# A state-space layer and a gated feed-forward in one kernel: the first loads, and the order of loads behind them, rearranged

## The chip, the cores and the metric

The kernel runs on one core of a Trainium2 chip. The metric is the device time of one execution in microseconds (us); of several runs the median counts. A core has five engines that run side by side, each with its own instruction queue: TensorE (PE in the profile, with its weight loads as PEld), VectorE (DVE), ScalarE (ACT), GpSimd (POOL) and SyncE (SP). Transfers between memory and the core are issued from SP, ACT or POOL and share 16 DMA engines.

## The reference

The first half is a chunked state-space layer over x [4 batches, 8 heads, 768 tokens, 32], a decay a per token, and B and C with 16 states per token. With L the causal products of decays inside a chunk, it computes:

```python
M = (C_chunk @ B_chunk.T) * L                       # chunk x chunk
y = M @ x_chunk + (C_chunk @ state) * exp(cum)      # inside, and from the state before
state = decay_full * state + (B_chunk * decay_from_j).T @ x_chunk
```

The heads are put side by side, which gives 3072 tokens of 256 features, and the second half is a gated feed-forward over d_ff = 1536:

```python
out = (np.maximum(y @ w_gate, 0) * (y @ w_val)) @ w_out
```

## The kernel before, in words

Tokens go through in 12 pairs of 128-token chunks (three pairs to a batch), and the feed-forward in 6 blocks of 512 tokens, two pairs to a block. The whole order is written out by hand: for each engine the last line (`in_order`, L798) chains the instructions in the order of the program text, so where a call stands in the text is where its instructions stand in each engine's queue.

The start. `a` is loaded as 64 rows (batch, head, half of the sequence) of 384 values, in two column pieces of 256 and 128 (L114 to L116, on SP). B and C of pair 0 are issued from ACT (`load_wide(0, nc.scalar)`, L117), x of pair 0 and B and C of pair 1 from SP behind a (L118, L119). A first activation (L122) brings ACT's table load. DVE, TensorE and POOL meanwhile set up zero tiles, identities and masks; `keep_warm(n)` (L159) issues n dummy matmuls on a zero tile, 14 of them first (L165). POOL issues the first six feed-forward weight transfers (L183 to L185; `weights(f0, f1)` brings columns f0 to f1, in units of 128, of w_gate and of w_val).

Decays are products, so `cp` is built by two multiplying scans over a, split at column 256 like the load (L189 to L193); the second scan starts from the first one's last value. `first_decay` (L217, called at L594) brings pair 0's decays to the token layout by matmuls that need only the first 256 columns. Then for pair 0: a reciprocal (L599), the scaling of B and of C by the decays (`first_scale`, L235, called at L600 and L601), dummies, the transposes of B and of C (`transp`, L323, called at L604 and L606), their copies out of PSUM (BT on ACT at L356, CT on DVE at L369), the matmul bu, which sorts B's rows (L608 to L611), the casts of x (L618), the scores (`G`, L371), their masking (`gevac`, L390), the state matmul (`astep`, L415) with its evacuation (`sevac`, L424), and the output (`first_y`, L439), from which the first feed-forward matmuls follow (`gvp`, L534; L544 is its matmul). The first state of pair 1 and the rest of pair 0 are computed in between.

Later pairs need their own factors: `wide_decay` (L198) is the matmul that brings them and `wide_factors` (L241) copies them and their reciprocals by DVE. `scale_bc` (L275) scales B and C on POOL and `cast_x` (L298) casts x. `load_wide(p, q, hold)` (L75) issues B and C of a pair; with `hold`, a one-element memset by DVE on the destination stands ahead of the transfers, and since they overwrite it, the queue waits with them until DVE has come that far. `load_x` (L87) issues x in two transfers and `load` (L97) all six of a later pair. Pairs 2 and 3 are loaded at L633 to L636, the last weights at L639 and L640, pairs 4 and 5 at L652.

PSUM is used through seven banks in turn (`bank`, L66), so a tile waits until the tile seven requests before it has been read. From `gvp(0, 0, 0)` (L642) on, feed-forward matmuls (`gvp`, `gv`, `gvh`, `fout`) are interleaved with the pieces of the next pairs.

Of the kernel before, what the change touches and what calls it, by code (L numbers as in the profile page):

```python
# [29 lines left out]
def kernel(  # L30
# [13 lines left out]
    nc = tc.nc  # L44
# [7 lines left out]
    NF = DF // 128  # L52
# [22 lines left out]
    def load_wide(p, q=nc.sync, hold=False):  # L75
        b, c0 = p // PPB, 2 * (p % PPB)
        sl = slice(c0 * 128, (c0 + 2) * 128)
        bcr = raw.tile([128, NH, 2, 2, N], FP32, tag="bcr", name="bcr")
        if hold:
            nc.vector.memset(bcr[0:1, 0, 0, 0, 0:1], 0.0)  # L80
        for src, j in ((B, 0), (C, 1)):
            q.dma_start(
                out=bcr[:, :, j].rearrange("p h r n -> p h (r n)"),
                in_=src[b, :, sl, :].rearrange("h (p r) n -> p h (r n)", r=2))
        st[p] = {"bcr": bcr}

    def load_x(p, hold=False):  # L87
        b, c0 = p // PPB, 2 * (p % PPB)
        xr = raw.tile([128, 2, NH, D], FP32, tag="xr", name="xr")
        if hold:  # L90
            nc.vector.memset(xr[0:1, 0, 0, 0:1], 0.0)
        for i in range(2):
            cs = slice((c0 + i) * 128, (c0 + i + 1) * 128)
            nc.sync.dma_start(out=xr[:, i], in_=x[b, :, cs, :].rearrange("h s d -> s h d"))
        st[p]["xr"] = xr
# [15 lines left out]
    H = S // 2  # L111
    HC = NC // 2
    a_sb = glob.tile([2 * BH, H], FP32)
    a_rows = a.rearrange("b h (w s) -> (b h w) s", w=2)  # L114
    for lo, hi in ((0, 256), (256, H)):
        nc.sync.dma_start(out=a_sb[:, lo:hi], in_=a_rows[:, lo:hi])  # L116
    load_wide(0, nc.scalar)  # L117
    load_x(0)  # L118
    load_wide(1)  # L119
    first = const.tile([1, 2], FP32)  # L120
    nc.vector.memset(first, 0.0)
    nc.scalar.activation(first[:, 1:2], first[:, 0:1], AF.Relu)  # L122
# [1 line left out]

    warm = const.tile([128, 256], BF16)
    nc.vector.memset(warm, 0.0)
    identf = const.tile([2 * BH, 2 * BH], FP32)
    make_identity(nc, identf)
    ident = const.tile([128, 128], BF16)
# [29 lines left out]
    def keep_warm(n, cols=256):  # L159
        w = bank("w")  # L160
        for _ in range(n):
            nc.tensor.matmul(out=w[:, 0:cols], lhsT=warm[:, 0:128], rhs=warm[:, 0:cols],  # L162
                             start=True, stop=True)
# [8 lines left out]
    def weights(f0, f1):  # L172
        fs = slice(f0 * 128, f1 * 128)
        for w, src in ((wg, moe_w_gate), (wv, moe_w_val)):
            nc.gpsimd.dma_start(
                out=w[:, :, fs], in_=src[:, fs].rearrange("(k p) f -> p k f", k=2))
# [12 lines left out]
    for lo, hi in ((0, 256), (256, H)):  # L189
        nc.vector.tensor_tensor_scan(  # L190
            out=cp[:, lo:hi], data0=a_sb[:, lo:hi],
# [6 lines left out]
    def wide_decay(ps):  # L198

        d = bank("wdec", (128, len(ps), 2, 8))  # L200
        first = True
        for k, p in enumerate(ps):
            b, c0 = p // PPB, 2 * (p % PPB)
            for i in range(2):
                w, o = (c0 + i) // HC, ((c0 + i) % HC) * 128
                for r in range(2):
                    nc.tensor.matmul(  # L207
                        out=d[64 * i:64 * i + 64, k, r],
                        lhsT=cp[:, o + r:o + 128:2], rhs=pick[:, w, 8 * b:8 * b + 8],
                        start=first or (k == 0 and r == 0), stop=True,  # L210
                        tile_position=(0, 64 * i), skip_group_check=True)
                first = False
        return d
# [27 lines left out]
    def wide_factors(ps, d):  # L241
        f = const.tile([128, len(ps), 2, 2, 8], FP32, name="wf%d" % ps[0])
        nc.vector.reciprocal(f[:, :, 0], d)
        nc.vector.tensor_copy(f[:, :, 1], d)
        for k, p in enumerate(ps):
            factors[p] = f[:, k].rearrange("p j r h -> p (j r) h")
# [27 lines left out]
    def scale(p, eng, ceng):  # L274
        scale_bc(p, eng)  # L275
        cast_x(p, ceng)

    def scale_bc(p, eng):
        b, c0 = p // PPB, 2 * (p % PPB)
        s = st[p]  # L280
        bs = att.tile([128, 4, 128], BF16, tag="bs", name="bs")
        if p < NWIDE:
            src = s["bcr"].rearrange("s h j r n -> s (j r) h n")
            f = factors[p]
        else:
            src = s["bcr"].rearrange("s i j h n -> s (i j) h n")
            f = scaleBC[:, b, c0:c0 + 2].rearrange("s c j h -> s (c j) h")
        eng.tensor_tensor(  # L288
            out=bs.rearrange("s k (h n) -> s k h n", h=NH), in0=src,
            in1=f.to_broadcast([128, 4, NH, N]), op=ALU.mult)  # L290
        if p < NWIDE:
            s["tin"] = [[bs[:, 2 * j + r] for r in range(2)] for j in range(2)]
            s["sort"] = s["tin"][0]
        else:
            s["tin"] = [[bs[:, 2 * i + j] for i in range(2)] for j in range(2)]
            s["B"] = s["tin"][0]
# [26 lines left out]
    def transp(p, k, apart=False):  # L323

        s = st[p]
        if "tp" not in s:
            s["tp"] = {}
        if apart and k == 1:
            s["tp"][k] = bank("tpc", (128, 2, 128), BF16)
        elif not s["tp"]:  # L330
            tp = bank("tp", (128, 2, 2, 128), BF16)
            s["tp"] = {0: tp[:, 0], 1: tp[:, 1]}
        for i in range(2):
            nc.tensor.transpose(out=s["tp"][k][:, i], in_=s["tin"][k][i], identity=ident)  # L334

    def tevac(p, beng, ceng):

        s = st[p]
        tp = s.pop("tp")
        s["BT"] = BT = att.tile([128, 2, 2, 128], BF16, tag="BT", name="BT")  # L340
        s["CT"] = CT = att.tile([128, 2, 128], BF16, tag="CT", name="CT")
        wide = p < NWIDE

        def tokens(k):
            src = tp[k]
            if wide:
                return src.rearrange("s r m -> s m r")
            return src.rearrange("s i m -> s (i m)")

        def rows(dst):  # L350
            dst = dst.rearrange("s i m -> s (i m)")
            return dst.rearrange("s (m r) -> s m r", r=2) if wide else dst

        if beng is nc.scalar:
            for t in range(2):
                nc.scalar.mul(rows(BT[:, t]), tokens(0), tmask[:, t:t + 1])  # L356
        else:
            src = tokens(0).unsqueeze(1)
            out_ = BT.rearrange("s t i m -> s t (i m)")
            if wide:  # L360
                shape = [128, 2, 128, 2]
                out_ = out_.rearrange("s t (m r) -> s t m r", r=2)
                mk = tmask.unsqueeze(2).unsqueeze(3)
            else:
                shape = [128, 2, 256]
                mk = tmask.unsqueeze(2)
            nc.vector.tensor_tensor(out=out_, in0=src.to_broadcast(shape),
                                    in1=mk.to_broadcast(shape), op=ALU.mult)
        (ceng.copy if ceng is nc.scalar else ceng.tensor_copy)(rows(CT), tokens(1))  # L369
# [45 lines left out]
    def astep(p, i):  # L415

        c = 2 * (p % PPB) + i
        if c == NC - 1:
            return
        nc.tensor.matmul(  # L420
            out=A_ps, lhsT=st[p]["B"][i], rhs=st[p]["x"][i],
            start=(c == 0), stop=(c == NC - 2), skip_group_check=True)
# [179 lines left out]
    s0["tin"] = [[bs0[:, 2 * j + r] for r in range(2)] for j in range(2)]  # L602
    keep_warm(5)
    transp(0, 0, True)  # L604
    keep_warm(1)
    transp(0, 1, True)  # L606
    tevac(0, nc.scalar, nc.vector)
    bu = bank("bu", (128, 128))  # L608
    for r in range(2):
        nc.tensor.matmul(out=bu, lhsT=order[:, 0, r], rhs=bs0[:, r],  # L610
                         start=(r == 0), stop=(r == 1))  # L611
    bxu = att.tile([128, 128], BF16, tag="bxu", name="bxu", bufs=1)
    nc.scalar.copy(out=bxu, in_=bu)
    s0["B"] = [bxu, None]
# [2 lines left out]
    for i in range(2):  # L617
# [3 lines left out]
    G(0)  # L621
    gevac(0, 4)
    astep(0, 0)
    d1 = wide_decay([1])
    keep_warm(5)
    sevac(0, 0)
    wide_factors([1], d1)
    scale_bc(1, nc.gpsimd)
    first_y()
    dm = first_mid()  # L630
    nc.vector.tensor_tensor(out=fB[:, 1], in0=fB[:, 0],
                            in1=dm.unsqueeze(1).to_broadcast([128, 2, 8]), op=ALU.mult)
    load_wide(2, nc.sync, True)  # L633
    load_x(2)
    load_wide(3)
    load_x(3)  # L636
    first_scale(0, fB[:, 1], bsm)
    s0["sort"] = [bsm[:, r] for r in range(2)]
    weights(6, 9)  # L639
    weights(9, NF)  # L640

    gvp(0, 0, 0)  # L642
    sort_b(0)
# [4 lines left out]
    astep(0, 1)  # L648
    sevac(0, 1)
    st.pop(0)  # L650
    cast_x(1, nc.gpsimd)
    for n in (4, 5):  # L652
        load(n, nc.sync)
    gvp(0, 0, 2)
    sort_evac(1)
    G(1)
# [2 lines left out]
    gevac(1, 3)  # L659
    sevac(1, 0)  # L660
    gvp_evac(*u)
    dall = decay()
    Dm(1)
    inter(1, 0)
# [2 lines left out]
    d2 = wide_decay([2, 3])  # L667
    yevac(1, nc.scalar)
    wide_factors([2, 3], d2)
    scale(2, nc.gpsimd, nc.gpsimd)  # L670
    sevac(1, 1)
    gvp(0, 1, 0)
# [156 lines left out]
```

## Time and profile before

| | |
|---|---|
| median of 3 runs | 129.77 us (129.56 to 132.0) |
| the profiled execution, its own time | 131.06 us |
| span of that execution in the profile | 129.4 us |
| mean granted clock of TensorE | 0.998 |
| TensorE busy | 124.6 us, 96% of the span |
| DVE, ACT, POOL busy | 88.0, 77.7 and 42.5 us |
| DMA | 12.11 MB, 94 GB/s in the mean |

The profile's times start at the span's beginning; 131.06 - 129.4 = 1.7 us of the execution lie outside the span. The chain of waits follows the work that ended last backwards, so a piece in it is one that the end waited for. The timeline lists instructions by start and length, with the idle time of the engine ahead of them and what ended it in brackets. Queues of DMA issues are written SPq, ACTq; L82 is line 82 of the kernel. Matmuls overlap, and their single lengths are longer than their distance.

### The profile page before, as it was taken

The page shows a single profiled execution, that of the slowest core. Times are in us where ns is not written, and L with a number is a line of the kernel's source. Part 1 is how long each engine was busy: PE and PEld are TensorE (multiplying, and loading weights), DVE is VectorE, ACT ScalarE, POOL GpSimd, SP SyncE. Part 2 cuts the span into 40 slices and gives each one's busy share as a digit, 9 for nine tenths or more (in the row PEclk, how much of TensorE's full clock was granted, in tenths as well). Part 3 has the DMA queues.
Part 4 walks back from the last instruction along what each step waited for, and adds up shares of the span by engine and source line. Part 5 has one row for each costly group of instructions (what it writes and reads, how often), then busy time and mean ns, then how long its engine had stood idle before and what let it go on. Part 6 is the DMA issues. An engine that isn't in the chain of part 4 may idle for free.

```text
span 129.4 us, 3381 instructions
## 1 busy us (share of the span) xinstructions
PE 124.6 (96%) x1290; PEld 89.5 (69%) x1290; DVE 88.0 (68%) x188; ACT 77.7 (60%) x167; POOL 42.5 (33%) x73
## 2 busy tenths in 40 slices
PE   6999999999999999999999999999999999999990
PEld 4566778458889888884468875478865488854780
DVE  6774767798987835277774876973896974687511
ACT  3061757888864544384944794935885844976410
POOL 7969545291803303900003750021920031100000
PEclk9999999999999999999999999999999999999999
DMA  3999999899950789879932099902200002200022
GB/s 73 165 202 165 166 204 151 121 112 142 192 62 3 97 99 118 258 144 105 126 36 82 34 149 119 113 3 81 85 6 0 0 5 81 81 0 0 5 81 81
DMA packets 74304, 12.11 MB, mean 94 GB/s; under 512 B 66992, under 2 KB 74288, under 8 KB 74288
## 3 DMA queue, kind: packets, MB, share of 16 engines
q1 hardware_dynamic: 67648, 9.02, 44.3%
q0 software_dynamic: 4272, 2.36, 13.9%
q10 hardware_dynamic: 2368, 0.52, 1.9%
q8 instruction: 10, 0.16, 0.5%
q14 instruction: 6, 0.05, 0.1%
HBM read 11.11 MB, written 3.15 MB: 110 GB/s over the span
## 4 chain that ended last, share of the span: by engine, by line
PE 92%; DVE 2%; DMA 2%; issue 0%; DVEq 0%
PE o L561 25%; PE gate L504 12%; PE val L507 12%; PE gv L527 11%; PE gate L544 7%; PE val L544 6%; PE y L471 4%; PE g L378 3%; PE A_ps L420 3%; PE w L162 2%; DMA a_sb<-in_a_dram 2%; PE y L461 2%; PE tp L334 2%; DVE h L516 1%; PE wdec L207 1%; PE bp L311 1%
## 5 line engine op out<-in xcount | busy, mean ns | idle before, releaser
L561 PE MATMUL o<-wo,h 128*128 128x256 bf16 x288 | 34.4, 273 | 0.0
L386 POOL TENSOR_SCALAR_AFFINE_SELECT gs<-gs 128x512 bf16<-128x512 bf16 (+1 forms) x27 | 13.9, 543 | 60.9 <-ACT gs L403 60.9
L561 PEld LDWEIGHTS <-h 128*128 128x128 bf16 x288 | 27.6, 98 | 5.1 <-DVE h L516 0.2
L516 DVE TENSOR_TENSOR h<-r,val 128x512 bf16<-128x512 bf16 x38 | 25.2, 684 | 7.0 <-ACT r L515 5.7
L410 DVE TENSOR_TENSOR gs<-g,maskUT 128x512 bf16<-128x512 f32 (+1 forms) x32 | 17.4, 592 | 11.3 <-issue 8.1
L515 ACT ACTIVATE r<-gate 128x512 bf16<-128x512 f32 x38 | 22.0, 608 | 3.7 <-PE gate L504 3.2
L504 PE MATMUL gate<-yT,wg 128*128 128x512 bf16 x76 | 22.6, 379 | 0.0
L507 PE MATMUL val<-yT,wv 128*128 128x512 bf16 x76 | 22.6, 379 | 0.0
L531 DVE TENSOR_TENSOR h<-r,gv 128x256 bf16<-128x256 bf16 x32 | 13.3, 421 | 6.4 <-ACT r L530 6.1
L403 ACT CAST gs<-g 128x512 bf16<-128x512 f32 (+1 forms) x27 | 12.0, 506 | 7.4 <-PE g L378 7.4
L553 DVE TENSOR_TENSOR h<-r,val 128x512 bf16<-128x512 bf16 x18 | 12.2, 686 | 4.2 <-ACT r L552 3.8
L507 PEld LDWEIGHTS <-wv 128*128 128x128 bf16 x76 | 7.4, 98 | 9.0
L552 ACT ACTIVATE r<-gate 128x512 bf16<-128x512 f32 x18 | 10.7, 603 | 4.5 <-PE gate L544 4.1
L530 ACT ACTIVATE r<-gv 128x256 bf16<-128x256 f32 x32 | 12.3, 385 | 1.1
L527 PE MATMUL gv<-yT,wg 128*128 128x256 bf16 x64 | 12.3, 273 | 0.0
L527 PE MATMUL gv<-yT,wv 128*128 128x256 bf16 x64 | 12.2, 273 | 0.0
L544 PE MATMUL gate<-yT,wg 128*128 128x256 bf16 x72 | 11.3, 281 | 0.0
L504 PEld LDWEIGHTS <-wg 128*128 128x128 bf16 x76 | 7.0, 98 | 6.1 <-issue 0.8
L544 PE MATMUL val<-yT,wv 128*128 128x256 bf16 x72 | 11.0, 276 | 0.0
L492 ACT CAST yT<-y 128x512 bf16<-128x512 f32 x11 | 6.5, 587 | 6.5 <-PE y L471 5.4
L577 ACT COPY ob<-o 128x512 f32<-128x512 f32 x10 | 5.9, 586 | 6.5 <-PE o L561 6.5
L288 POOL TENSOR_TENSOR bs<-bcr,scaleBC 128x512 bf16<-128x512 f32 x8 | 8.5, 1062 | 3.8 <-DMA bcr<-in_C_dram 3.3
(93 smaller groups left out, 144.6 us busy)
## 6 DMA issues: line engine op xcount, KB each, us to landing
xr<-in_x_dram SPq DMA_DIRECT2D x24, 128.0 KB, 3.3
out_dram<-ob SPq DMA_DIRECT2D x10, 256.0 KB, 2.7
bcr<-in_B_dram SPq DMA_DIRECT2D x16, 64.0 KB, 3.0
bcr<-in_C_dram SPq DMA_DIRECT2D x16, 64.0 KB, 3.0
wo<-in_moe_w_out_dram POOLq DMA_DIRECT2D x1, 768.0 KB, 8.9
bcr<-in_B_dram SPq DMA_DIRECT2D x3, 128.0 KB, 4.6
wg<-in_moe_w_gate_dram POOLq DMA_DIRECT2D x3, 128.0 KB, 4.8
wv<-in_moe_w_val_dram POOLq DMA_DIRECT2D x3, 128.0 KB, 4.7
```

The costliest lines, as they stand in the source:

```text
L386: nc.gpsimd.affine_select(out=dst, in_=dst, pattern=[[0, n], [1, 128]], compare_op=ALU.is_ge, fill=0.0, base=0, channel_multiplier=-1)
L410: nc.vector.tensor_tensor(out=d[:, q, h], in0=g[q][:, h], in1=m[:, h], op=ALU.mult)
L504: nc.tensor.matmul(out=g, lhsT=wg[:, k, fs], rhs=yT[:, k, tk], start=(k == 0), stop=(k == 1))
L507: nc.tensor.matmul(out=v, lhsT=wv[:, k, fs], rhs=yT[:, k, tk], start=(k == 0), stop=(k == 1))
L515: nc.scalar.activation(r, g, AF.Relu)
L516: nc.vector.tensor_tensor(out=fst[b][:, f], in0=r, in1=v, op=ALU.mult)
L527: nc.tensor.matmul(out=gv_[:, j], lhsT=w[:, k, fs], rhs=yT[:, k, tk], start=(k == 0), stop=(k == 1), skip_group_check=True)
L530: nc.scalar.activation(r, gv_[:, 0], AF.Relu)
L531: nc.vector.tensor_tensor(out=fst[b][:, f, u * 256:(u + 1) * 256], in0=r, in1=gv_[:, 1], op=ALU.mult)
L544: nc.tensor.matmul(out=o[:, j], lhsT=w[:, k, fs], rhs=yT[:, k, tk], start=(k == 0), stop=(k == 1), skip_group_check=True)
L553: nc.vector.tensor_tensor(out=fst[b][:, f:f + 2, u * 256:(u + 1) * 256], in0=r, in1=v, op=ALU.mult)
L561: nc.tensor.matmul(out=o[:, ts % 2], lhsT=fst[b][:, f, ts * 128:(ts + 1) * 128], rhs=wo[:, f], start=(f == 0), stop=(f == NF - 1), skip_gr ...
```

## The change

It moves loads, and a few steps near the start; what is computed stays the same.

- a comes by one transfer of 384 columns. The two scans stay split.
- B and C of pair 0, x of pair 0, and B and C of pair 1 are issued behind the first activation and the memset of `warm` in the text; B and C of pair 0 with `hold`, so behind a memset by DVE.
- One dummy between the transposes of pair 0 is gone, and bu stands ahead of C's transposes.
- Pair 1's `wide_decay` stands behind five dummies, not ahead of them.
- Pair 2's loads stand right behind pair 1's factors, pair 3's behind the factors of pairs 2 and 3 (with `hold`), followed by pairs 4 and 5. Pair 1's cast of x on POOL takes the place of the last weights, and these stand behind pair 1's masks.

```diff
     a_sb = glob.tile([2 * BH, H], FP32)
-    a_rows = a.rearrange("b h (w s) -> (b h w) s", w=2)
-    for lo, hi in ((0, 256), (256, H)):
-        nc.sync.dma_start(out=a_sb[:, lo:hi], in_=a_rows[:, lo:hi])
-    load_wide(0, nc.scalar)
-    load_x(0)
-    load_wide(1)
+    nc.sync.dma_start(out=a_sb, in_=a.rearrange("b h (w s) -> (b h w) s", w=2))
     first = const.tile([1, 2], FP32)
     nc.vector.memset(first, 0.0)
     nc.scalar.activation(first[:, 1:2], first[:, 0:1], AF.Relu)
...
     warm = const.tile([128, 256], BF16)
     nc.vector.memset(warm, 0.0)
+    load_wide(0, nc.scalar, True)
+    load_x(0)
+    load_wide(1)
...
     keep_warm(5)
     transp(0, 0, True)
-    keep_warm(1)
-    transp(0, 1, True)
-    tevac(0, nc.scalar, nc.vector)
     bu = bank("bu", (128, 128))
     for r in range(2):
         nc.tensor.matmul(out=bu, lhsT=order[:, 0, r], rhs=bs0[:, r],
                          start=(r == 0), stop=(r == 1))
+    transp(0, 1, True)
+    tevac(0, nc.scalar, nc.vector)
...
     astep(0, 0)
+    keep_warm(5)
     d1 = wide_decay([1])
-    keep_warm(5)
     sevac(0, 0)
     wide_factors([1], d1)
+    load_wide(2, nc.sync, True)
+    load_x(2)
     scale_bc(1, nc.gpsimd)
     first_y()
...
-    load_wide(2, nc.sync, True)
-    load_x(2)
-    load_wide(3)
-    load_x(3)
     first_scale(0, fB[:, 1], bsm)
     s0["sort"] = [bsm[:, r] for r in range(2)]
     weights(6, 9)
-    weights(9, NF)
+    cast_x(1, nc.gpsimd)
...
     st.pop(0)
-    cast_x(1, nc.gpsimd)
-    for n in (4, 5):
-        load(n, nc.sync)
     gvp(0, 0, 2)
...
     gvp_evac(*u)
+    weights(9, NF)
     dall = decay()
...
     wide_factors([2, 3], d2)
+    load_wide(3, nc.sync, True)
+    load_x(3)
+    for n in (4, 5):
+        load(n, nc.sync)
     scale(2, nc.gpsimd, nc.gpsimd)
```

## The prediction

> **What bounds the kernel now.** I read the head of the page first, then the chain of waits from 0 to 14 us, then the timeline of the same stretch.
>
> ```profile
> span 129.4 us, 3381 instructions
> PE 124.6 (96%) x1290; PEld 89.5 (69%) x1290; DVE 88.0 (68%) x188; ACT 77.7 (60%) x167; POOL 42.5 (33%) x73
> PEclk9999999999999999999999999999999999999999
> ```
>
> TensorE is busy for 96% of the span. Whatever the change moves on another engine is worth time only where TensorE now waits for it, and 129.4 - 124.6 leaves 4.8 us of idle TensorE in the whole kernel.
>
> ```profile
> 0.81 2.88 DMA a_sb<-in_a_dram
> ...
> 4.54 0.61 PE fdec L222 x8
> ...
> 6.64 0.21 PE w L162
> ...
> 8.58 0.54 PE wdec L207 x8
> 9.12 1.18 PE w L162 x5
> 10.30 0.55 PE y L471 x16
> ...
> 11.70 0.97 PE gate L544 x4
> 12.67 0.60 PE val L544 x4
> ```
>
> Columns: start, length, what. Three things are to be seen. The chain begins with the transfer of a and its first scan: 3.7 us in which nothing else can go on. From 4.5 to 11.7 us the chain stands on TensorE, but the w rows are dummies on a zero tile, so this stretch is a latency chain filled up, not work. From 11.70 the feed-forward matmuls run, and from there TensorE is the bound. So the change can gain or lose (a) at the start, up to 11.7 us, and (b) later only by delaying something past the moment TensorE wants it.
>
> ```profile
> 0.81 0.47 ACTq L82 DMA_DIRECT2D bcr<-in_B_dram  x1
> 0.81 1.20 SPq L116 DMA_DIRECT2D a_sb<-in_a_dram  x2
> ...
> 0.94 0.17 DVE L126 MEMSET warm<- 128x128 uint32 x1
> ...
> 1.16 3.17 PE L162 MATMUL w<-warm 128*128 128x256 bf16 x14 [1.16 <-DVE tmask L136]
> ...
> 1.30 0.60 ACTq L82 DMA_DIRECT2D bcr<-in_C_dram  x1
> ...
> 1.94 1.28 ACT L122 ACT_TABLE_LOAD   x1 [1.94 <-issue]
> ...
> 3.23 0.20 ACT L122 ACTIVATE first<-first 1x1 f32<-1x1 f32 x1
> ...
> 3.71 0.68 DVE L190 TENSOR_TENSOR_SCAN cp<-a_sb,zero 64x256 f32<-64x256 f32 x1 [0.46 <-DMA a_sb<-in_a_dram]
> ...
> 4.50 0.48 DVE L190 TENSOR_TENSOR_SCAN cp<-a_sb,cp,zero 64x128 f32<-64x128 f32 x1
> ...
> 5.35 0.35 DVE L599 RECIPROCAL wf<-fdec 128x16 f32<-128x16 f32 x1
> ...
> 5.76 0.43 DVE L236 TENSOR_TENSOR bs<-bcr,wf 128x256 bf16<-128x256 f32 x1
> ...
> 6.11 0.41 DVE L236 TENSOR_TENSOR bs<-bcr,fdec 128x256 bf16<-128x256 f32 x1
> ...
> 6.68 0.84 ACT L356 ACTIVATE BT<-tp,tmask 128x256 bf16<-128x256 bf16 x2 [3.25 <-PE tp L334]
> ...
> 9.96 0.25 DVE L243 RECIPROCAL wf<-wdec 128x16 f32<-128x16 f32 x1
> ...
> 11.11 0.42 DVE L452 CAST yT<-y 128x256 bf16<-128x256 f32 x1 [0.86 <-PE y L448]
> ```
>
> **The change, part by part.**
>
> *One transfer of a.* Two issues took 1.20 us on SP, so one takes about 0.6 and the queue's next issues (x of pair 0, then B and C of pair 1) go 0.6 us earlier.
>
> ```profile
> a_sb<-in_a_dram SPq DMA_DIRECT2D x1, 64.0 KB, 2.9
> a_sb<-in_a_dram SPq DMA_DIRECT2D x1, 32.0 KB, 3.0
> bcr<-in_B_dram ACTq DMA_DIRECT2D x1, 128.0 KB, 3.0
> bcr<-in_C_dram ACTq DMA_DIRECT2D x1, 128.0 KB, 3.2
> bcr<-in_B_dram SPq DMA_DIRECT2D x3, 128.0 KB, 4.6
> ```
>
> The last column is the time from issue to landing. 32, 64 and 128 KB took 2.9 to 3.2 us, so size hardly counts at this point and 96 KB should take 2.9 as well. The late bound is the landing of the second piece now, 0.81 + 0.60 + 3.0 = 4.41: the first scan would start 0.7 us later than at 3.71. The early bound is TensorE: the 14 dummies end at 1.16 + 3.17 = 4.33 and fdec starts at 4.54, so at most 0.2 us is there. I take the landing where it is (3.7, nearest to the 64 KB row, which left at the same moment). What is gained surely is the gap between the scans: the first ends at 3.71 + 0.68 = 4.39, the second starts at 4.50, because its piece lands at 4.41. DVE then runs without a break from the second scan to the reciprocal at 5.35 and the two scalings at 5.76 and 6.11, so this 0.1 us goes through: -0.1, between -0.2 and +0.7.
>
> *B and C of pair 0.* They move behind a one-element memset on DVE (behind `warm`, so done at about 0.94 + 0.17 + 0.06 = 1.17) and, in ACT's order, behind the table load and the first activation. Now they land at 0.81 + 3.0 = 3.81 and 1.30 + 3.2 = 4.50 and are wanted at 5.76 and 6.11: a cover of 1.95 and 1.61 us. If ACT's queue issues them while the table load runs, B leaves at about 1.25 and C 0.49 later, 0.44 us later than now, and both stay covered; even at the 4.6 us of the loaded row, C lands at 1.74 + 4.6 = 6.34, which costs 0.2. If they wait for the activation's end, B leaves at 0.81 + 1.28 + 0.20, about 2.3, and C at 2.8; then C lands between 2.8 + 3.2 = 6.0 (nothing lost) and 2.8 + 4.6 = 7.4 (1.3 lost). I take 0: no row shows ACT's queue behind a running instruction, and the cover holds in all but the late part of this. The bounds are 0 and +1.3. The Trainium skill, PSUM — Partial Sum Buffer, Engine vs sequencer instructions, says that a sequencer's own instruction waits for earlier ones only until they are dispatched, not until they end; if DMA issues count as such, that is the early case, and nothing in this trace shows it either way. Against the change speaks ScalarE: Activation LUTs, What ACT_TABLE_LOAD costs, in the Trainium skill: a table load of 1.28 us and a drain of 1.38 behind it; an estimate by that page would issue B at about 3.5 and C at about 4.0, landing at 7.2 at best, 1.1 us late. The trace agrees with the 1.28 but shows the activation 0.01 us behind the load, with no drain between.
>
> *One dummy less, bu ahead of C's transposes.* The 0.21 us in the chain is shade: C's transposes wait for DVE's scaling, which ends at 6.11 + 0.41 = 6.52, and bu's two matmuls now fill that place. G waits for BT, 6.68 + 0.84 = 7.52. I cost it at 0, between -0.2 (if it had held up G) and 0. The shared banks move up by one place with it, and each later tile follows the same tile as before.
>
> *Pair 1's decays behind the dummies.* On TensorE 0.54 and 1.18 change places; y still starts at 10.30. On DVE the reciprocal now waits for wdec's end at 10.30: about 10.5 instead of 9.96, plus the copy and a memset until about 10.9. The next on DVE is the cast of yT at 11.11: covered by 0.2 us, and without that cover the first gate would start late by as much. On POOL the scaling of pair 1 slides from 10.32 to about 11.
>
> ```profile
> 10.32 1.05 POOL L288 TENSOR_TENSOR bs<-bcr,wf 128x512 bf16<-128x512 f32 x1 [0.17 <-DVE wf L244]
> ...
> 16.25 1.58 POOL L386 TENSOR_SCALAR_AFFINE_SELECT gs<-gs 128x512 bf16<-128x512 bf16 x3 [1.40 <-ACT gs L403]
> ...
> 19.69 1.06 POOL L288 TENSOR_TENSOR bs<-bcr,wf 128x512 bf16<-128x512 f32 x1 [1.86 <-DVE wf L244]
> ...
> 25.76 0.59 PE L507 MATMUL val<-yT,wv 128*128 128x512 bf16 x2
> 38.48 1.06 POOL L288 TENSOR_TENSOR bs<-bcr,scaleBC 128x512 bf16<-128x512 f32 x1 [3.30 <-DMA bcr<-in_C_dram]
> ```
>
> ```profile
> 45.71 0.22 PE tp L334 x4
> ```
>
> ```profile
> wv<-in_moe_w_val_dram POOLq DMA_DIRECT2D x1, 192.0 KB, 6.1
> ```
>
> It ends at about 12.1, and its transposes run behind the val matmuls of 12.67 + 0.60, at 13.3: 1.2 us of cover. 0.
>
> *Loads.* Pair 2's four transfers leave SP about a microsecond earlier (hold at about 10.9). On POOL, pair 1's cast takes the place of the last weights. These go behind the masks of pair 1, 16.25 + 1.58 = 17.83, and take 2 x 0.7 us until 19.3, just ahead of the scaling at 19.69. The last wv leaves at about 18.6, and even at the slowest landing of its kind, 6.1, it is there at 24.7; gv(0, 9) wants it at 25.76. 0, with 1.0 us of cover. Pair 3's loads now wait for the decays of pairs 2 and 3 (about 19.6, the moment of the POOL row at 19.69), and pairs 4 and 5 queue behind them on SP. The one scaling that already waits for such a load, at 38.48, may slide by about half a microsecond; its transposes come at 45.71: 45.71 - 38.48 - 1.06 = 6.2 us of cover. 0.
>
> The sum is -0.1 us. The profiled execution took 131.06 us, so this gives 130.96 for it; it stands 1.29 above the median of 129.77, and for the median I forecast 129.7.
>
> **The rivals.**
>
> *B and C stand behind the table load (slower).* One mechanism: the ACT queue issues nothing until the activation has ended. For it speaks that ACT did its issues and its load strictly one after the other (1.30 + 0.60, then 1.94); against it, that an issue ahead of a load says nothing of one behind it. It decides from the point where C lands later than 6.11; between the bounds 0 and 1.3 its likely price is 0.6: 130.3 to 130.4.
>
> *TensorE's rate turns at another moment (either side).* The five dummies take 1.18 us, 0.236 each, and four gate matmuls of the same width at 11.70 take 0.97, 0.24 each; later ones run at half of that.
>
> ```profile
> 14.35 0.44 PE gate L544 x4
> ```
>
> So the doubling came near 12.7, although the granted clock stands at full. If it came when y starts, 10.30, the 2.4 us up to 12.7 would shrink by half of their matmul work, 0.55 + 0.97 of it at least: -0.8, 129.0. If it came as much later, about +0.8: 130.6. The change leaves the string of matmuls from 8.6 us unbroken, which speaks against a shift; but less filling around 7 us could move it. The Trainium skill, TensorE: Matmul & The Clock Gate, Part 1, tells of a free-running window of about 3.4 us that has to be busy before the rate doubles, so that the moment varies between runs of one kernel; no trace here shows more than one such moment.
>
> *The last weights come late (slower).* If the denser loads from 19.6 us stretch their landing by 2 us over the slowest row, gv(0, 9) waits 24.7 + 2 - 25.76, about 0.9: 130.6. Against it speaks that pair 2's loads have left the queues by then.
>
> *It is hidden anyway.* If the scans are not held up by the second piece's landing, nothing changes: 129.8. That lies inside the forecast.
>
> **How the numbers follow.** Forecast (129.4 to 130.0, hidden anyway included): 0.55. B and C behind the table load: 0.23. The rate earlier: 0.08; later: 0.07. Late weights: 0.04. Something else: 0.03. The time is that of the first, 129.7. The range reaches to the early rate with the early bound of a, 129.7 - 0.8 - 0.2 = 128.7, and to the late bound of C, 129.77 + 1.3 = 131.1. A measurement of this kernel can tell about 2%, 2.6 us, from no change. No case alone reaches that: faster 0.02 (several gains at once), slower 0.04 (late C together with a late rate), within 0.94.
>
> **What would show it.** Right: the chain still begins with a's transfer of about 2.9 us, the second scan follows the first without a gap, the ACT issues of B and C start near 1.3 us during the table load, the scaling of C starts near 6.0, gate L544 near 11.6, and TensorE's busy time stays at 124 to 125 us. Wrong: an idle time of DVE ahead of L236 that a bcr transfer ends, ACT issues only after 2.3 us, an idle time of TensorE ahead of gv(0, 9) at 25 us, or a first scan later than 4 us.

## The result, and the profile after

The changed kernel takes 129.56 us in the median of 22 executions (129.21 to 130.05); the kernel before, measured beside it, takes 130.29 us in the median of 22 (129.56 to 132.12). The ratio is 0.9951, 95% interval 0.9931 to 0.9972: within 2%, and a little faster. The ratios leave out executions that lie more than 1.5% above the fastest of their kernel (in pe_order, for one, the six above 131 us); since some of those turn out to matter, the table of the experiments counts every execution, but for three of 181 to 686 us.

The head of the page of the changed kernel, whose profiled execution took 129.54 us against 131.06 before:

```profile
span 127.8 us, 3378 instructions
PE 122.4 (96%) x1289; PEld 88.7 (69%) x1289; DVE 87.9 (69%) x190; ACT 77.5 (61%) x167; POOL 42.4 (33%) x73
```

The span is 1.6 us shorter, TensorE's busy time 2.2 us, with one matmul less. So most of the difference between these two executions is not waiting, it is the same matmuls taking less time. The chain of waits shows where (start, length, what), with two lines of the kernel before behind it:

```profile
1.17 3.15 PE w L160 x14
4.33 0.09 issue
4.41 0.60 PE fdec L220 x8
5.01 1.18 PE w L160 x5
6.20 0.21 PE tp L332 x2
6.41 0.21 PE bu L605 x2
...
7.35 0.43 PE g L376 x16
...
9.70 0.29 PE y L469 x6
...
10.66 0.60 PE gate L542 x4
11.26 0.44 PE val L542 x4
...
12.78 0.44 PE gate L542 x4
```

```profile
7.28 0.43 PE w L162 x2
7.71 0.55 PE g L378 x16
```

fdec starts 0.13 us earlier than before (4.41 for 4.54), G 0.36 (7.35 for 7.71), the first gate 1.04 (10.66 for 11.70). Most of the last is no wait that went: TensorE's rate doubled at about 7.3 us here, between bu at the slow pace and G, and at about 12.7 in the profile before. The rate is read from the distance between the starts of two matmuls of 256 columns: 0.21 us while it is slow, 0.11 us after the doubling. The same five dummies, the last one's end included, took 1.25 us ahead of the doubling and 0.71 behind it:

```profile
4.95 1.25 PE L160 MATMUL w<-warm 128*128 128x256 bf16 x5
...
7.81 0.71 PE L160 MATMUL w<-warm 128*128 128x256 bf16 x5
```

From the second set of gates to the end of the span both executions take the same time (129.4 - 14.35 = 115.05 before, 127.8 - 12.78 = 115.02 here). So the whole 1.6 us is made ahead of it. The timeline of the same execution, for the steps of the prediction:

```profile
0.80 1.28 ACT L117 ACT_TABLE_LOAD   x1 [0.80 <-PEq L810]
0.81 0.56 SPq L114 DMA_DIRECT2D a_sb<-in_a_dram  x1
...
1.16 0.44 ACTq L82 DMA_DIRECT2D bcr<-in_B_dram  x1
...
1.63 0.66 ACTq L82 DMA_DIRECT2D bcr<-in_C_dram  x1
...
3.25 0.19 DVE L149 COPY pick<-identf 64x32 f32<-64x32 f32 x1
3.58 0.68 DVE L188 TENSOR_TENSOR_SCAN cp<-a_sb,zero 64x256 f32<-64x256 f32 x1
...
4.30 0.48 DVE L188 TENSOR_TENSOR_SCAN cp<-a_sb,cp,zero 64x128 f32<-64x128 f32 x1
...
5.43 0.42 DVE L234 TENSOR_TENSOR bs<-bcr,wf 128x256 bf16<-128x256 f32 x1
...
5.77 0.41 DVE L234 TENSOR_TENSOR bs<-bcr,fdec 128x256 bf16<-128x256 f32 x1
...
16.92 0.72 POOL L173 DMA_DIRECT2D wv<-in_moe_w_val_dram  x1
...
24.19 0.59 PE L505 MATMUL val<-yT,wv 128*128 128x512 bf16 x2
```

ACT issued B and C while its table load was running. The scalings stand without a gap behind what DVE does ahead of them, so DVE did not wait for B and C. It waited 0.14 us for a: it was free at 3.25 + 0.19 = 3.44, a landed 2.8 us behind its issue at 0.81, and the first scan started at 3.58. The last wv left at 16.92 for a matmul at 24.19.

### The profile page after: what moved, and what is told of

It is laid out like the page before. It is cut to its first block, busy times and chain, and to the rows that moved or that the text cites. A ratio compares the mean times of both kernels' runs of the same rounds, so it can differ in the third digit from the quotient of the medians.

```text
span 127.8 us, 3378 instructions
## 1 busy us (share of the span) xinstructions
PE 122.4 (96%) x1289; PEld 88.7 (69%) x1289; DVE 87.9 (69%) x190; ACT 77.5 (61%) x167; POOL 42.4 (33%) x73
## 4 chain that ended last, share of the span: by engine, by line
PE 92%; DVE 3%; POOL 1%; ACT 1%; issue 1%; DVEq 0%
PE o L559 25%; PE gate L502 12%; PE val L505 12%; PE gv L525 11%; PE gate L542 7%; PE val L542 6%; PE w L160 3%; PE y L469 3%; PE g L376 3%; PE A_ps L418 2%; PE y L459 2%; PE tp L332 1%; DVE h L514 1%; POOL gs L384 1%; PE bp L309 1%; PE dec L252 1%
## 5 line engine op out<-in xcount | busy, mean ns | idle before, releaser
L542 PE MATMUL gate<-yT,wg 128*128 128x256 bf16 x72 | 10.8, 273 | 0.1
```

Of the source, the lines that this page charges most:

```text
L542: nc.tensor.matmul(out=o[:, j], lhsT=w[:, k, fs], rhs=yT[:, k, tk], start=(k == 0), stop=(k == 1), skip_group_check=True)
```

## The experiments

Each kernel was run 12 times, beside 33 or 35 executions of the kernel before on the same chip: one call for the first four, one for the second four, one for the last four. The changed kernel's 22 executions from the first measurement are in the table too.

| kernel | median us | ratio (95%) | below 129.75 | 129.75 to 130.6 | above 130.6 | rate doubles at, us |
|---|---|---|---|---|---|---|
| before, beside the first four | 129.58 | | 21 | 8 | 4 | |
| start_loads | 129.37 | 0.998 (0.996 to 1.001) | 9 | 3 | 0 | 7 |
| pe_and_decays | 130.30 | 1.003 (1.000 to 1.006) | 4 | 4 | 4 | 4 |
| late_loads | 129.56 | 1.000 (0.998 to 1.003) | 8 | 2 | 2 | 14 |
| before, beside the second four | 129.98 | | 16 | 10 | 9 | |
| after_again | 129.31 | 0.996 (0.995 to 0.998) | 12 | 0 | 0 | 4 |
| a_one | 130.15 | 1.002 (1.000 to 1.005) | 3 | 8 | 1 | 11 |
| gap_filled | 129.53 | 0.998 (0.996 to 1.001) | 9 | 3 | 0 | 6 |
| gap_widened | 129.80 | 1.003 (0.999 to 1.006) | 4 | 4 | 4 | 14 |
| before, beside the last four | 129.94 | | 16 | 18 | 1 | |
| bc_late | 129.61 | 0.999 (0.997 to 1.001) | 8 | 4 | 0 | 7 |
| pe_order | 130.60 | 0.998 (0.996 to 1.001) | 5 | 1 | 6 | 14 |
| decays_behind | 129.51 | 1.000 (0.997 to 1.002) | 7 | 4 | 1 | 5 |
| scan_free | 129.29 | 0.999 (0.996 to 1.001) | 9 | 2 | 1 | 4 |
| the change, first measurement | 129.56 | 0.995 (0.993 to 0.997) | 18 | 4 | 0 | 7 |

The kernel before falls into three groups: near 129.5, near 130.1 and near 131.4 (in the second call 16, 10 and 9 executions with means of 129.51, 130.13 and 131.46). Of the changed kernel's 34 executions none lies in the highest group and 30 in the lowest; the other four, all of the first measurement, lie between 129.79 and 130.05. The share of the highest group in the kernel before differs from call to call (7 of 22, 4 of 33, 9 of 35, 1 of 35), so counts are best compared within a call. The columns' bounds are fixed: the eight executions of gap_widened below 130.6 lie close together, at 129.57 to 129.85.

The last column is read from where the distance between matmuls halves in the one profile of each, and these profiles say what the highest group is. The five profiled executions above 130.6 us (131.06 for the kernel before, 130.67 for a_one, 131.53, 131.20 and 131.42 for late_loads, gap_widened and pe_order) are the five in which the rate doubled later than 10 us. The other eight doubled by 7.3 us; seven of them took 129.20 to 129.54, and the eighth, bc_late, 130.34.

**The theories.** *Chain*: the path from a's landing to the first gate is shorter, the rest is chance. *Rate*: the change alters how often TensorE's rate doubles early. A third, that later loads compete less, was tested with late_loads.

**before_again**, the kernel before. 

> The kernel before, unchanged. Theory chain (the change shortens the path from a's landing to the first gate by about 0.3 us, and the rest of the difference between the two profiles is chance): ratio 1.00, and in the profile TensorE's rate doubles at any moment, say 7 to 13 us. Theory rate (the change makes the doubling come early in nearly every execution, where it comes at a varying moment before): ratio 1.00 as well, and single times from 129.5 to 132; its own profile may show the five dummies ahead of the first y at 0.59 or at 1.18 us.


Measured 0.999 (0.996 to 1.002), 9 executions at 129.4 to 130.0 and two at 131.4. It repeats; the twelfth, which has the profile, took 685.6 us and is not used.

**start_loads**

```diff
-    for lo, hi in ((0, 256), (256, H)):
-        nc.sync.dma_start(out=a_sb[:, lo:hi], in_=a_rows[:, lo:hi])
-    load_wide(0, nc.scalar)
-    load_x(0)
-    load_wide(1)
+    nc.sync.dma_start(out=a_sb, in_=a.rearrange("b h (w s) -> (b h w) s", w=2))
...
     nc.vector.memset(warm, 0.0)
+    load_wide(0, nc.scalar, True)
+    load_x(0)
+    load_wide(1)
```

> The kernel before with only the start's loads changed: one transfer of a, and B and C of pair 0, x of pair 0 and B and C of pair 1 behind the memset. Theory chain: G starts about 0.35 us earlier (7.35 in place of 7.71) and the time is 0.3 us lower, ratio 0.997, with single times spread as before. Theory rate: if the smaller gap ahead of fdec is what matters, the rate doubles near 7.3 us, single times lie between 129.2 and 130.1, ratio 0.995. A theory of later loads (less competition from 11 us on) gives 1.000.


The median fell by 0.2 us beside the kernel before, the ratio's interval takes in 1, and no execution lies above 130.3 where the kernel before had 4 of 33 above 130.6. G starts at 7.20. That this part of the change keeps the late executions away is likely and not shown: by the share of the kernel before, one or two of 12 were to be expected. Three executions lie in the middle group.

**pe_and_decays**

```diff
     transp(0, 0, True)
-    keep_warm(1)
-    transp(0, 1, True)
-    tevac(0, nc.scalar, nc.vector)
     bu = bank("bu", (128, 128))
...
+    transp(0, 1, True)
+    tevac(0, nc.scalar, nc.vector)
...
+    keep_warm(5)
     d1 = wide_decay([1])
-    keep_warm(5)
```

> The kernel before with only TensorE's order changed: one dummy less, bu ahead of C's transposes, pair 1's decays behind the five dummies. Theory chain: no change, ratio 1.000, G at 7.7 us. Theory rate: if the order of the dummies is what matters, the doubling comes early in nearly every execution and single times lie in a band of 0.9 us, ratio 0.996; if it is the gap at the start, 1.000 and a wide band.


Neither: the ratio is 1.003, its interval just above 1, and 8 of 12 executions lie above 129.75. TensorE's order is not free, which the chain theory had it be; and it is not what makes the change fast.

**late_loads**

```diff
     wide_factors([1], d1)
+    load_wide(2, nc.sync, True)
+    load_x(2)
...
-    load_wide(2, nc.sync, True)
-    load_x(2)
-    load_wide(3)
-    load_x(3)
...
-    weights(9, NF)
+    cast_x(1, nc.gpsimd)
...
-    cast_x(1, nc.gpsimd)
-    for n in (4, 5):
-        load(n, nc.sync)
...
+    weights(9, NF)
...
     wide_factors([2, 3], d2)
+    load_wide(3, nc.sync, True)
+    load_x(3)
+    for n in (4, 5):
+        load(n, nc.sync)
```

> The kernel before with only the loads behind the start changed: pair 2 earlier, pairs 3, 4 and 5 and the last weights later, pair 1's cast earlier on POOL. Theories chain and rate: ratio 1.000 within 0.3%, and no idle time of TensorE between 12 and 60 us. A theory of less competition gives 0.995.


1.000, as chain and rate had it. By itself this part is worth nothing that shows, and it takes neither the middle nor the highest group away.

**after_again**, the changed kernel. 

> The changed kernel as it is, beside the others on one chip. Both theories: single times within 129.2 to 130.1 and ratio 0.995 to 0.998. Theory rate: none above 130.3, and the rate doubles before 8 us in the profile; theory chance: a few above 130.3, as the kernel before has.


All 12 lie between 129.14 and 129.57, while 19 of 35 executions of the kernel before on the same chip lie above 129.75. Together with the first measurement none of 34 is above 130.6; of the kernel before, 14 of 103 beside the experiments and 7 of 22 in the first measurement are.

**a_one**

```diff
-    for lo, hi in ((0, 256), (256, H)):
-        nc.sync.dma_start(out=a_sb[:, lo:hi], in_=a_rows[:, lo:hi])
+    nc.sync.dma_start(out=a_sb, in_=a.rearrange("b h (w s) -> (b h w) s", w=2))
```

> The kernel before with one transfer of a and nothing else (B and C of pair 0 stay at the front of ACT's queue). Theory chain: a lands where its first piece did, the second scan follows without a gap, 0.1 us lower, ratio 0.999; if the competing transfers of B and C are what held a, a lands no earlier than 3.7. Theory rate: the gap ahead of fdec stays at about 0.2 us, so single times above 130.3 stay as frequent as before.


Slower, 1.002 (1.000 to 1.005). The chain of waits of this kernel:

```profile
0.81 3.40 DMA a_sb<-in_a_dram
4.23 0.69 DVE cp L188
...
5.06 0.60 PE fdec L220 x8
```

The one transfer took 3.40 us beside B and C, the scan started 0.5 us later than before and all behind it moved. Issue to landing, in this kernel and then in the changed one, where B and C leave 0.35 us later:

```profile
bcr<-in_B_dram ACTq DMA_DIRECT2D x1, 128.0 KB, 3.7
bcr<-in_C_dram ACTq DMA_DIRECT2D x1, 128.0 KB, 3.6
a_sb<-in_a_dram SPq DMA_DIRECT2D x1, 96.0 KB, 3.4
```

```profile
bcr<-in_B_dram ACTq DMA_DIRECT2D x1, 128.0 KB, 2.9
bcr<-in_C_dram ACTq DMA_DIRECT2D x1, 128.0 KB, 3.9
a_sb<-in_a_dram SPq DMA_DIRECT2D x1, 96.0 KB, 2.8
```

So the same 96 KB land 0.6 us sooner when they start alone; in the four other profiles with the changed start they took 2.6 to 2.7 us. TensorE meanwhile idles ahead of fdec:

```profile
5.06 0.60 PE L220 MATMUL fdec<-identf,cp 64*64 64x8 f32 x8 [0.74 <-DVE cp L188]
```

In spite of this gap one of 12 executions lies above 130.6, where the kernel before had 9 of 35. The rate theory expected as many as before.

**gap_filled**

```diff
-    keep_warm(14)
+    keep_warm(16)
```

> The kernel before with 16 dummies at the front in place of 14, which fills the gap between the dummies and fdec (4.33 to 4.54 us) and nothing else. Theory rate, with the gap as its cause: single times above 130.3 vanish, median down by 0.1 to 0.6 us, the doubling before 8 us in the profile. Theory chain: no change or 0.05 us more, times above 130.3 as frequent as before.


No execution above 130.4, median 0.45 us below that of the kernel before; the ratio, 0.998 (0.996 to 1.001), does not settle it. Of 12 executions at the kernel before's share in this call (9 of 35), three would have been above 130.6. It goes the way of the rate theory and is not enough by itself.

**gap_widened**, the changed kernel with

```diff
-    keep_warm(14)
+    keep_warm(10)
```

> The changed kernel with 10 dummies at the front in place of 14, so that TensorE idles about 0.9 us longer ahead of fdec, which waits for a's scan anyway. Theory rate: late doublings come back, single times from 129.3 to 131.5, median up by 0.3 to 1 us, and the profile may show the doubling near 10 to 13 us. Theory chain: the path runs over a and the scan, so the time stays at 129.5.


4 of 12 above 130.6 (130.98 to 131.63), where the changed kernel had none in the same call. The chain of waits of its profile:

```profile
4.34 0.61 PE fdec L220 x8
...
7.28 0.61 PE g L376 x15
...
8.22 1.07 PE w L160 x5
...
11.22 0.97 PE gate L542 x4
12.19 0.85 PE val L542 x4
13.04 0.43 PE bp L309 x4
```

Its fdec and its G start no later than in the changed kernel (4.34 for 4.41, 7.28 for 7.35), so the waits are as short as there. But the five dummies, the gates and bp all run at the slow pace, up to about 14 us. The dummies at the front do no work, and four fewer of them bring the late executions back: that is the rate theory's prediction, and the chain theory has no place for it. Against the 12 of after_again in the same call, 4 to 0 could still be chance; against all 34 of the changed kernel it hardly is. Only one of the four has a profile.

**bc_late**: start_loads without the first hunk's new line, so a stays in two transfers.

> The kernel before with B and C of pair 0, and the loads behind them, moved as in the change, but a still in two transfers. Theory competition (a lands when it does because B and C of pair 0 flow beside it): the first piece of a lands before DVE is free, at 3.4 us or earlier, the first scan starts then, and the time falls as with both edits, ratio 0.997, no single time above 130.4. Theory one transfer (the single transfer is what helps): the first scan stays at 3.7 and the ratio is 1.000.


The scans start at 3.30 and 4.09 (DVE's timeline):

```profile
3.30 0.68 DVE L190 TENSOR_TENSOR_SCAN cp<-a_sb,zero 64x256 f32<-64x256 f32 x1
4.09 0.48 DVE L190 TENSOR_TENSOR_SCAN cp<-a_sb,cp,zero 64x128 f32<-64x128 f32 x1
```

That is earlier than with the one transfer: holding back B and C is what brings a in sooner, not the single transfer. The time was less good than expected, 0.999. Its profiled execution, at 130.34 us, lies in the middle group, and shows two waits that start_loads (129.51 us, one transfer of a, the same later loads, doubled at 7 us as well) does not have. The chain of waits, POOL, DVE and TensorE:

```profile
12.26 7.50 DMA bcr<-in_C_dram
```

```profile
10.40 1.05 POOL L288 TENSOR_TENSOR bs<-bcr,wf 128x512 bf16<-128x512 f32 x1 [0.90 <-DMA bcr<-in_C_dram]
...
19.92 1.05 POOL L288 TENSOR_TENSOR bs<-bcr,wf 128x512 bf16<-128x512 f32 x1 [3.42 <-DMA bcr<-in_C_dram]
```

```profile
10.61 1.12 DVE L236 TENSOR_TENSOR bsm<-bcr,wf 128x256 bf16<-128x256 f32 x1
```

```profile
11.78 0.38 PE L311 MATMUL bp<-bsm,order 128*128 128x128 bf16 x4 [0.24 <-DVE bsm L236]
...
21.03 0.29 PE L334 MATMUL tp<-ident,bs 128*128 128x128 bf16 x2 [0.46 <-POOL bs L288]
```

The same scaling by DVE in start_loads:

```profile
10.61 0.43 DVE L234 TENSOR_TENSOR bsm<-bcr,wf 128x256 bf16<-128x256 f32 x1
```

First, two transfers of a hold SP's queue longer: C of pair 1 leaves at 4.82, and at 3.84 in start_loads. POOL's scaling of pair 1 waits for it until 10.40 and then runs beside DVE's scaling, which takes 1.12 us in place of 0.43; bp starts at 11.78 and not at 11.38. So the single transfer has a use of its own, behind the start. Second, C of pair 2 is still on its way when TensorE comes to that pair (7.50 us from issue to landing), POOL waits for it and TensorE idles 0.46 us. Together they are about the difference of the spans, 128.6 for 127.8 us. In the changed kernel C of pair 2 leaves SP at 11.79, not at 12.26, the last weights are out of its way, and POOL's scaling at 18.13 does not wait for a transfer:

```profile
18.13 1.05 POOL L286 TENSOR_TENSOR bs<-bcr,wf 128x512 bf16<-128x512 f32 x1 [0.49 <-DVE bcr L80]
```

**pe_order**: the first half of pe_and_decays' diff (one dummy less, bu ahead). 

> The kernel before with one dummy less and bu ahead of C's transposes, nothing else. Theory rate: if less filling near 6.5 us delays the doubling, single times above 130.2 in half the executions and a ratio of 1.003; if the decays' place did it, 1.000. Theory chain: 1.000.


6 of 12 at 131.3 to 131.5, the highest share of all and the reason for the median of 130.60; the kernel before had 1 of 35 in the same call. As the rate theory had it: with one dummy of 0.21 us less, and bu in its new place, the early doubling is rarer. Which of the two does it was not tried. The changed kernel has this edit too and no such execution in 34, so the rest of the change more than makes up for it.

**decays_behind**: the second half. 

> The kernel before with pair 1's decays behind the five dummies, nothing else. Theory rate: the dummies stand closer to G, so the doubling is at least as early as before; ratio 0.998 to 1.000. If this edit is what made the late executions of the run with both edits, 1.003. Theory chain: 1.000.


1.000 and one execution above 130.6, at 130.61: this half is free, so the late executions in pe_and_decays come from the first half.

**scan_free**, the changed kernel with

```diff
     for q in range(4):
...
-        nc.vector.tensor_copy(
+        nc.scalar.copy(
             smask[r, q // 2, c:c + 64].rearrange("p (t d) -> p t d", t=2),
...
-    keep_warm(14)
+    keep_warm(13)
```

> The changed kernel with the four casts that build smask moved from DVE to ACT, so that DVE is free when a lands, and 13 dummies at the front in place of 14. Theory competition: a lands before 3.4 us, the first scan starts at its landing with an idle time ahead of it, near 3.3, fdec 0.1 to 0.3 us earlier, ratio to the kernel before 0.994 to 0.996. If a lands at 3.4 or later after all, the scan stays at 3.45 and the ratio at 0.996.


A miss, in DVE's timeline:

```profile
3.48 0.68 DVE L188 TENSOR_TENSOR_SCAN cp<-a_sb,zero 64x256 f32<-64x256 f32 x1 [1.54 <-DMA a_sb<-in_a_dram]
```

DVE was free 1.54 us earlier and waited; a lands at about 3.46 and not before 3.4, so DVE's masks were hardly in the way. 0.999 (0.996 to 1.001), median 129.29: no version beat the changed kernel by anything that shows. One of 12, with its 13 dummies, lies at 130.95.

## Why the prediction was right, and where it was off

The time lies in the range and within 2% of before, as forecast. The forecast was a gain of 0.1 us against the median then known; the medians of 22 executions differ by 0.7, so the sign held and the size was too small. That 129.7 comes so near the measured 129.56 is in part luck: it was reckoned from a median of three executions, 129.77, where 22 of the same kernel gave 130.29, and most of the gain came from a rival. Of the six signs that were to show the mechanism, two came: the second scan follows the first without a gap, and the ACT issues start near 1.3 us during the table load. C's scaling came a little early, at 5.77 for 6.0. Three did not come: the chain of the changed profile runs back from fdec over the dummies and not over a's transfer, the gate starts at 10.66 and not near 11.6, and TensorE is busy for 122.4 us, not 124 to 125. Step by step:

*One transfer of a.* Right in its path, wrong as a step of its own: "size hardly counts at this point and 96 KB should take 2.9 as well" held for the number, 2.8, but only because B and C left later. With them at the front it took 3.4, near the late bound. I had read the landing times as fixed and missed that the rows of B, C and a were three transfers in flight at once. The gap between the scans went as said, and it counts: the reciprocal starts 0.85 us behind the second scan in every profile. But the term of 0.1 us was too small. The second scan starts at 4.40 to 4.60 in the six profiles with the old start and at 4.11 to 4.30 in the five with the changed one, about 0.3 us earlier, because a lands sooner as well. The prediction also named the queue's earlier issues: bc_late, which lacks them, gets C of pair 1 late.

*B and C of pair 0.* Right: issued at 1.16 and 1.63, during the table load of 0.80 to 2.08, and not waited for. The rival that they stand behind the table load fell. By the rule of the Trainium skill, PSUM — Partial Sum Buffer, Engine vs sequencer instructions, if it covers DMA issues, these had only to wait for the dispatch; the trace agrees, with an issue 0.92 us before the load's end. The cover shrank more than said: C took 3.9 us and landed 0.26 us ahead of its scaling. What I left out is the gain: their delay of 0.35 us is what lets a land sooner.

*One dummy less.* Wrong at "I cost it at 0", in two ways. "G waits for BT" misread the chain: BT and CT were copied by 7.53 (7.11 + 0.42), and G stood behind two dummies until 7.71, so the step's own bound of -0.2 was the nearer price. And pe_order, which has this step alone, puts half its executions at 131.4.

*Decays behind the dummies.* Right at 0: decays_behind gave 1.000 (0.997 to 1.002).

*Loads.* The covers held in the changed kernel: the last wv left 7.3 us ahead of its matmul, and TensorE worked 47.97 of the 48 us from 12 to 60. But the covers were worked out where the rate doubles late, as in the profile that I had. Where it doubles early, the old order can let TensorE wait for C of pair 2, as in bc_late; start_loads, pe_and_decays, gap_filled and decays_behind, with the old order and an early doubling too, show no such wait. What makes the middle group stays open: late_loads, with the new order, and the changed kernel in its first measurement have executions there as well.

*The rate as a rival.* The mechanism was right, its chance and its place were wrong. I gave it 0.15 in all and wrote that the change "leaves the string of matmuls from 8.6 us unbroken, which speaks against a shift"; the doubling came ahead of that string, at 7.3 us, and the change moves how often it comes early. In the second call the means of before and after are 130.19 and 129.32, 0.87 apart. That 9 of 35 executions no longer pay 1.95 us is worth 0.50 of it, over half, and this is the rate's. That 10 of 35 no longer pay 0.62 is worth 0.18, and its cause is open. The lowest group fell from 129.51 to 129.32, 0.19 us. The shorter path may be that, or an earlier doubling inside the group: the two profiled executions of the changed kernel took 129.54 us, doubling at 7.3, and 129.20, doubling at 4. So the prediction's sum, which has only the path in it, can stand for no more than this last part.

What stays open is what sets the moment of the doubling. The profiles show it at 4 to 7.3 us or at 10.5 to 14 us and none between. Idle time ahead of fdec alone does not set it: the profile of pe_and_decays has 0.23 us there and doubled by 4.5 us, the one of pe_order has none and doubled at 14, and a_one, with 0.74 us, has few late executions. Nor is it enough that TensorE is kept busy. In the profile of the kernel before (stretch, length, TensorE's busy time, granted clock, DMA share and GB/s)

```profile
4.54:8.00 3.46, 3.46 (x38) 1.00 1.29 171
8.00:11.00 3.00, 3.00 (x44) 1.00 1.45 197
11.00:12.60 1.60, 1.60 (x9) 1.00 1.05 160
```

TensorE was busy for 8.06 us in a row, and the rate had not doubled. The Trainium skill, TensorE: Matmul & The Clock Gate, Part 1, tells of a free-running window of about 3.4 us that must be busy. If busy means matmuls without a break, this trace does not agree, since 8.06 us hold at least one whole window. No run here varied the window's phase on purpose.

## What to carry to other kernels

Look at single execution times before reading one profile: where they fall into groups, a profile shows one of them. A cover worked out where TensorE's rate doubles late can be gone where it doubles early, because everything that waits for TensorE's pace comes earlier there. And here the transfer that the kernel starts with landed sooner when what was not yet wanted left a third of a microsecond after it.

## What the runs showed of the hardware that was not expected

- 96 KB took 3.4 us from issue to landing beside two 128 KB transfers of another queue, issued at the same moment and 0.5 us later (a_one), and 2.6 to 2.8 us where the first of these left 0.35 us behind (five profiles).
- ACT's queue issued transfers at 1.16 and 1.63 us while a table load of 1.28 us ran from 0.80.
- DVE's scaling of 128x256 took 0.43 us by itself, and 1.12 us where POOL's scaling ran beside it (bc_late).
- TensorE's matmuls kept half rate until 4 to 14 us, at a granted clock shown as full. With four dummies fewer at the front, 0.86 us of idle time ahead of fdec, 4 of 12 executions of the changed kernel fell into the late group, with them none of 34.
